# The opening of a convolution and gated projection kernel: earlier casts, copies split by token blocks, and unit 1 convolved in other PSUM banks

## The chip, the cores and the metric

The kernel runs on one core of one Trainium2 chip. The metric is the device time of one execution in microseconds (us); the profile's span, from the first to the last instruction, is about 2 us shorter. In the text PE is TensorE, PEld its weight loads, ACT ScalarE, DVE VectorE, POOL GpSimd, and SP the engine whose queue issues most DMAs. [...]

## The reference

```python
# x: 8 x 4096 x 192, weight: 8 x 7, w_in: 192 x 2048, w_out: 2048 x 192
w = softmax(weight)                                  # per head, over 7 taps
x_pad = concatenate([zeros(B, 6, D), x], axis=1)
attn[b, s, h, :] = sum_k w[h, k] * x_pad[b, s + k, h, :]    # causal convolution, 24 channels a head
h = attn.reshape(32768, 192) @ w_in
out = (h * cos(h)) @ w_out                           # 32768 x 192, float32
```

## The kernel before

**Tiles and units.** The 32,768 tokens are cut into 32 units of 1,024 tokens and 64 tiles of 512 (`T`). A unit is loaded and convolved as a whole and feeds two tiles. The convolution is a matrix product: for each head a band matrix (`band`, 128 x 256 for the current block of 128 tokens and the block before it) holds the softmaxed taps on its diagonals. Its result `ct` has tokens on partitions; it is cast to bf16, doubled so that both halves of the partitions hold it after transposing (`double_unit`, on POOL), and transposed by DMA (`turn_unit`) into `cT`, with channels on partitions.

**A tile.** `mm1(t, j)` (L313) makes two of the sixteen blocks of 128 hidden features in a buffer `h` of two PSUM banks, from six matmuls. `gcu` (L325) takes the cosine on ACT (L327, a sine with a shifted phase) and the product with h on DVE (L331). `mm2_step` (L337) multiplies the products of the tile before by `w_out`, in the banks `o_ps0` and `o_ps1`; `evac` copies them out on ACT, and `store` sends them to memory.

**PSUM.** `h_pool` is a ring of three buffers of two banks; the other two banks are `o_ps0` and `o_ps1`. In the kernel before, the convolution takes its buffers from the h ring (L217).

**Order by hand.** Each engine works its instructions in the order in which the code gives them; waits come from the data dependencies and from buffers that have to come free. In a tile, `PE_ORDER` and `ACT_ORDER` (L368) spell the order: hN is mm1 of pair N, mN are N steps of the second projection, c1 and c2 (for tile 0 also d1 and d2) are the two halves of the matmuls of a half unit's convolution (`conv_part`, L214), sN is `gcu` of pair N, ec and ed are the copies of that convolution's result into `ct`, and | is the middle, at which transposes, stores and loads are issued. Tiles 0 and 1 have orders of their own (L371). In tile 0 the whole of unit 1 is convolved: d is its heads 0 to 3, c its heads 4 to 7. Behind its | come `double_unit(1)` and the casts of unit 2 to bf16 (`cast_unit`, L172: three instructions, and a copy of the margin, L181). In tile 1, c is the first half of unit 2.

**The opening.** While the first loads run, PE does matmuls on zeros (`keep_warm`, L93). ACT and DVE compute the softmax of the taps; DVE multiplies it with a mask into `prod` (L137) and adds seven planes of it (L140); eight copies of 32 partitions each, shared by DVE, ACT and POOL, bring the result into `band` (L147). Then x of unit 0 is cast, the first half on ACT, the second on POOL (L185 to L187). `conv_first` convolves unit 0 in two halves of four blocks: in each half and for each group of four heads, ACT copies one bank of the result into `ct` and DVE the other (`conv_out`, L204). The first half is transposed on PE (`turn_first`, L276), the second by DMA. Then the first half of w_in is cast (L297, one third on each of POOL, DVE and ACT), and the remaining casts go to POOL: the other half of w_in (L303), x of unit 1, and w_out (L306).

Of the kernel before, what the change touches and what calls it, by code (L numbers as in the profile page):

```python
# [8 lines left out]
FP32 = mybir.dt.float32  # L9
BF16 = mybir.dt.bfloat16  # L10
AF = mybir.ActivationFunctionType
ALU = mybir.AluOpType
# [4 lines left out]
def kernel(  # L17
# [8 lines left out]
    nc = tc.nc  # L26
    B, S, D = x.shape
    H, K = weight.shape
    Dff = moe_w_in.shape[1]
    G = D // H  # L30
    NTOK = B * S
    T = 512
    NT = NTOK // T
    NB = T // 128
    U = 1024
    NU = NTOK // U
    UB = U // 128
# [4 lines left out]
    NC = D // 64  # L42
    R = G // NC
# [3 lines left out]
    consts = ctx.enter_context(tc.tile_pool(name="consts", bufs=1))  # L47
# [7 lines left out]
    h_pool = ctx.enter_context(tc.tile_pool(name="h_ps", bufs=3, space=PSUM))  # L55
    o_pools = [ctx.enter_context(tc.tile_pool(name=n, bufs=1, space=PSUM)) for n in ("o_p", "o_q")]
# [18 lines left out]
    w_f = consts.tile([128, NC, NP, 128], FP32)  # L75
# [38 lines left out]
    for q in range(1, 4):  # L114
# [17 lines left out]
    winv = consts.tile([128, H, 1], FP32)  # L132
    nc.vector.reciprocal(winv, wsum)
    nc.vector.tensor_tensor(out=wn, in0=wexp, in1=winv.to_broadcast([128, H, K]), op=ALU.mult)

    prod = consts.tile([128, K, H, E], BF16)
    nc.vector.tensor_tensor(out=prod, in0=mask.rearrange("p k (o e) -> p k o e", o=1).to_broadcast([128, K, H, E]),  # L137
                            in1=wn.rearrange("p h (k o) -> p k h o", o=1).to_broadcast([128, K, H, E]), op=ALU.mult)
    for d, n, m in ((0, 3, 3), (0, 1, 1), (2, 1, 4), (0, 1, 2)):
        nc.vector.tensor_tensor(out=prod[:, d : d + n], in0=prod[:, d : d + n], in1=prod[:, d + m : d + m + n], op=ALU.add)  # L140


    copies = [nc.vector.tensor_copy, nc.scalar.copy, nc.gpsimd.tensor_copy]
    for odd in range(2):
        for q in range(4):
            e0 = 32 * (q ^ (2 * odd))
            copies[(4 * odd + q) % 3](out=band[32 * q : 32 * q + 32, odd:H:2, e0 : e0 + E],  # L147
                                      in_=prod[32 * q : 32 * q + 32, 0, odd:H:2, :])

    w = consts.tile([128, NC, NP, 128], BF16)  # L150
    wo = consts.tile([128, NP, 2, D], BF16)

# [19 lines left out]
    def cast_unit(u, n0=0, n1=UB):  # L172
        copy = nc.scalar.copy if u == 0 and n0 == 0 else nc.gpsimd.tensor_copy
        if u == 0:
            bf[u] = xb0
        else:
            bf[u] = xbf_pool.tile([128, UB + 1, D], BF16, name="x_bf")
            if u % UPS == 0:
                nc.gpsimd.memset(bf[u][:, 0, :], 0.0)
            else:  # L180
                nc.gpsimd.tensor_copy(out=bf[u][:, 0, :], in_=bf[u - 1][:, UB, :])  # L181

        o = bf[u][:, n0 + 1 : n1 + 1, :].rearrange("p n (h t k r) -> t p (n h) k r", t=2, k=NC, r=R)
        i = x_tiles[u][:, n0:n1, :].rearrange("p n (h t r k) -> t p (n h) k r", t=2, k=NC, r=R)
        copy(out=o[0], in_=i[0])  # L185
        copy(out=o[1, 0:64], in_=i[1, 64:128])  # L186
        copy(out=o[1, 64:128], in_=i[1, 0:64])  # L187
        bf.pop(u - 2, None)

    ct_tiles = {}  # L190

    def conv_view(ps, n):

        return ps[:, :, 0 : n * 2 * G].rearrange("p b (n k i r) -> p b i n k r", n=n, k=NC, i=2)

    def conv_mm(u, c, pv, i, rows, prev, n0, n1, **flags):
        h = 4 * c + i
        return nc.tensor.matmul(  # L198
            out=pv[:, i // 2, i % 2],
            lhsT=band[rows, h, 128 if prev else 0 : 256 if prev else 128],  # L200
            rhs=bf[u][rows, n0 + 1 - prev : n1 + 1 - prev, h * G : (h + 1) * G].rearrange("p n (k r) -> p n k r", k=NC),
            skip_group_check=True, **flags)

    def conv_out(u, c, ps, n0, n1, copies, double=False):  # L204
        for b in range(2):
            w0 = (2 * c + b) * 2 * R
            o = ct_tiles[u][:, n0:n1, :, :, w0 : w0 + 2 * R].rearrange("p n k t w -> p (n k) t w")
            i = ps[:, b, 0 : (n1 - n0) * 2 * G].rearrange("p (m t w) -> p m t w", t=1, w=2 * R)
            if double:
                copies[b](o, i.to_broadcast([128, (n1 - n0) * NC, 2, 2 * R]))  # L210
            else:
                copies[b](o[:, :, 0, :], i[:, :, 0, :])  # L212

    def conv_part(u, c, n0=0, n1=UB):  # L214


        ps = h_pool.tile([128, 2, T], FP32, name="h")  # L217
        pv = conv_view(ps, n1 - n0)
        sides = [slice(0, 64), slice(64, 128)]

        def mm(i, rows, prev=0, **flags):
            return conv_mm(u, c, pv, i, sides[rows], prev, n0, n1, **{"start": False, "stop": False, **flags})


        mm(0, 0, start=True)
        mm(2, 1, start=True)
        mm(1, 0)
        mm(2, 1, 1)
        m = mm(1, 0, 1)
        turn = Turn()  # L230
        turn.mark(m, mm(3, 1))
        yield
        m = mm(2, 0)
        turn.wait(m, mm(0, 1))
        mm(3, 0)
        mm(0, 1, 1)
        mm(3, 0, 1, stop=True)
        mm(1, 1, stop=True)
        yield
        if c == 0 and u not in ct_tiles:  # L240
            ct_tiles[u] = ct_pool.tile([128, UB, NC, 2, 64], BF16, name="ct")
        conv_out(u, c, ps, n0, n1, [nc.scalar.copy] * 2)
        yield

    cT = {}
# [13 lines left out]

    cast_unit(0, 0, NB)  # L260
    cast_unit(0, NB, UB)
    ct_tiles[0] = ct_pool.tile([128, UB, NC, 2, 64], BF16, name="ct")
    cT[0] = cT_pool.tile([128, UB, NC, 128], BF16, name="cT")
    copies = [nc.scalar.copy, nc.vector.tensor_copy]

    def conv_first(n0, n1):
        for c in range(2):
            ps = h_pool.tile([128, 2, T], FP32, name="h")
            for i in range(4):
                for prev in range(2):  # L270
                    conv_mm(0, c, conv_view(ps, NB), i, slice(0, 128), prev, n0, n1,
                            start=prev == 0 and i % 2 == 0, stop=prev == 1)
            yield
            conv_out(0, c, ps, n0, n1, copies, double=n0 == 0)

    def turn_first(half):  # L276
        ps = h_pool.tile([128, 2, T], FP32, name="h")
# [14 lines left out]
    list(b)  # L292
    for half in range(2):
        list(across[half])
    cast = [nc.gpsimd.tensor_copy, nc.vector.tensor_copy, nc.scalar.copy]
    for k in range(NC):
        cast[k](out=w[:, k, 0:HP], in_=w_f[:, k, 0:HP])  # L297
    double_unit(0, NB, UB)
    turn_unit(0, NB, UB)
    for q in range(2):  # L300
# [67 lines left out]
    PE_ORDER = "h0 c1 m8 c2 h1 m8 h2 h3 m16 | h4 h5 m8 h6 m12 h7 m12"  # L368
    ACT_ORDER = "P s0 ec s1 s2 s3 Q s4 s5 s6 s7"

    PE_FIRST = ["h0 h1 h2 h3 h4 h5 h6 d1 h7 d2 c1 c2 |", "h0 m8 h1 m8 h2 h3 m16 | h4 c1 h5 m8 c2 h6 m12 h7 m12"]  # L371
    ACT_FIRST = ["s0 s1 s2 s3 s4 s5 s6 ed s7 ec", "s0 s1 s2 s3 s4 s5 ec s6 s7"]

    for t in range(NT + 2):
        u, second = divmod(t, TPU)
        cu, cc = (u + 2, 0) if second else (u + 1, 1)
        conv = {"c": conv_part(cu, cc) if cu < NU else iter(())}
        if t == 0:
            conv["d"] = conv_part(1, 0)
        act, done, h, step = (ACT_ORDER if t > 1 else ACT_FIRST[t]).split(), set(), {}, 0  # L380

        def flush():
            while act:
                k = act[0]
                need = {"P": "start", "Q": "|", "e": k[1:] + "2"}.get(k[0], "h" + k[1:])
                if need not in done:
                    return
                act.pop(0)
                if k == "P" and 0 <= t - 2 < NT:
                    evac(t - 2, 0)  # L390
                elif k == "Q" and 0 <= t - 2 < NT:
                    evac(t - 2, 1)
                elif k[0] == "e":
                    next(conv[k[1]], None)
                elif k[0] == "s" and t < NT:
                    gcu(t, int(k[1:]), h.pop(int(k[1:])))

        done.add("start")
        flush()
        for k in (PE_ORDER if t > 1 else PE_FIRST[t]).split():  # L400
            if k[0] == "h" and t < NT:
                h[int(k[1:])] = mm1(t, int(k[1:]))
            elif k[0] in conv:
                next(conv[k[0]], None)
            elif k[0] == "m":
                for q in range(step, step + int(k[1:])):
                    mm2_step(t, q)
                step += int(k[1:])
            done.add(k)
            flush()  # L410

            if k == ("|" if t == 0 else "h1") and second == 0 and cu < NU:
                double_unit(cu)
            if k == "|":
                if second == 0 and cu < NU:
                    turn_unit(cu)
                if 0 <= t - 2 < NT:
                    store(t - 2)
                if second == 1 and u + 3 < NU:
                    load_unit(u + 3)  # L420
                if second == 0 and u + 2 < NU:
                    cast_unit(u + 2)
# [30 lines left out]
```

## Time and profile before

The time is 740.4 us, the median of three executions from 740.13 to 740.62; the profiled execution has a span of 738.2 us at a granted PE clock of 0.998.

| engine | busy, us | share of the span |
|---|---|---|
| PE | 723.3 | 98% |
| DVE | 620.2 | 84% |
| ACT | 626.8 | 85% |
| POOL | 177.7 | 24% |

The opening in the timelines:

| what | from, us | to, us |
|---|---|---|
| prod and its adds on DVE (L137, L140) | 5.02 | 8.99 |
| copies into band on three engines (L147) | 9.02 | 10.0 |
| casts of unit 0 (ACT; POOL runs beside it from 9.86) | 10.03 | 12.17 |
| convolution of unit 0 without a stop (L198) | 12.22 | 14.29 |
| casts of w_in's first half on ACT, then DVE (L297) | 15.50 | 17.62 |
| first projection (L321), but for two matmuls at 16.25 | 17.68 | |
| first product on DVE (L331) | 19.55 | |

A line of a timeline or of a group of instructions gives the start and the time in us, the engine, the line of the program, the operation, what it writes and reads with the shapes, and the number of instructions joined in it. In square brackets stands how long the engine had been idle before, and which instruction it waited for. A busy time is an average over stages with different limits; the chain of waits says what the end hung on.

### The profile page before, as it was taken

The page shows a single profiled execution, that of the slowest core. Times are in us where ns is not written, and L with a number is a line of the kernel's source. Part 1 is how long each engine was busy: PE and PEld are TensorE (multiplying, and loading weights), DVE is VectorE, ACT ScalarE, POOL GpSimd, SP SyncE. Part 2 cuts the span into 40 slices and gives each one's busy share as a digit, 9 for nine tenths or more (in the row PEclk, how much of TensorE's full clock was granted, in tenths as well). Part 3 has the DMA queues.
Part 4 walks back from the last instruction along what each step waited for, and adds up shares of the span by engine and source line. Part 5 has one row for each costly group of instructions (what it writes and reads, how often), then busy time and mean ns, then how long its engine had stood idle before and what let it go on. Part 6 is the DMA issues. An engine that isn't in the chain of part 4 may idle for free.

```text
span 738.2 us, 26755 instructions
## 1 busy us (share of the span) xinstructions
PE 723.3 (98%) x12073; PEld 553.9 (75%) x12073; DVE 620.2 (84%) x534; ACT 626.8 (85%) x781; POOL 177.7 (24%) x177
## 2 busy tenths in 40 slices
PE   6899999999999999999999999999999999999997
PEld 2477777777777777777777777777777777777776
DVE  6788888888888888888888888888888888888883
ACT  4788888888888888888888888888888888888883
POOL 5622202222212222212222202222212222211000
PEclk9999999999999999999999999999999999999999
DMA  7644244344255354244245244244245455333301
GB/s 188 176 109 112 84 130 119 79 131 117 80 130 125 72 129 124 77 127 129 74 124 130 76 122 129 78 119 130 77 119 131 83 114 114 101 112 87 88 24 66
DMA packets 167940, 79.96 MB, mean 108 GB/s; under 512 B 99474, under 2 KB 167058, under 8 KB 167826
## 3 DMA queue, kind: packets, MB, share of 16 engines
q1 hardware_dynamic: 167824, 78.26, 40.6%
q8 instruction: 94, 1.54, 0.9%
q14 instruction: 20, 0.16, 0.1%
q10 hardware_dynamic: 2, 0.00, 0.0%
HBM read 28.31 MB, written 25.17 MB: 72 GB/s over the span
## 4 chain that ended last, share of the span: by engine, by line
PE 94%; ACT 0%; issue 0%; SPq 0%
PE o_ps L347 46%; PE h L321 44%; PE h L198 4%; ACT o_sb L359 0%; SPq L161 0%
## 5 line engine op out<-in xcount | busy, mean ns | idle before, releaser
L331 DVE TENSOR_TENSOR g<-h,cs 128x1024 bf16<-128x1024 f32 x512 | 609.0, 1220 | 99.1 <-ACT cs L327 90.4
L327 ACT ACTIVATE cs<-h 128x1024 bf16<-128x1024 f32 x512 | 511.6, 1025 | 79.3 <-PE h L321 77.9
L347 PEld LDWEIGHTS <-g 64*128 64x128 bf16 x8192 | 362.1, 94 | 67.4 <-SPq L161 1.8
L347 PE MATMUL o_ps<-wo,g 64*128 64x192 bf16 x8192 | 409.0, 243 | 1.2 <-ACT o_sb L359 1.2
L321 PE MATMUL h<-cT,w 64*128 64x512 bf16 x3072 | 402.9, 377 | 4.1 <-DVE g L331 1.7
L321 PEld LDWEIGHTS <-w 64*128 64x128 bf16 x3072 | 166.1, 94 | 89.0 <-issue 6.4
L249 POOL COPY ct<-ct 128x1536 bf16<-128x1536 bf16 (+1 forms) x32 | 46.2, 1444 | 495.5 <-issue 489.4
L359 ACT COPY o_sb<-o_ps 128x384 f32<-128x384 f32 x128 | 61.3, 479 | 10.9 <-PE o_ps L347 8.2
L212 ACT CAST ct<-h 128x384 bf16<-128x384 f32 (+1 forms) x126 | 54.0, 480 | 11.0 <-PE h L198 7.1
L198 PE MATMUL h<-x_bf,band 64*128 64x192 bf16 (+1 forms) x776 | 55.3, 241 | 4.1 <-ACT x_bf L185 1.7
L198 PEld LDWEIGHTS <-band 64*128 64x128 bf16 (+1 forms) x776 | 38.0, 94 | 17.6 <-issue 3.2
L186 POOL CAST x_bf<-x_f 64x768 bf16<-64x768 f32 (+1 forms) x32 | 38.7, 1208 | 2.0
L187 POOL CAST x_bf<-x_f 64x768 bf16<-64x768 f32 (+1 forms) x32 | 38.5, 1204 | 1.9
L185 POOL CAST x_bf<-x_f 128x768 bf16<-128x768 f32 (+1 forms) x32 | 38.9, 1217 | 0.1
L95 PE MATMUL o_ps<-zero 128*128 128x512 bf16 x19 | 7.3, 554 | 1.3 <-DVE zero L90 1.3
L181 POOL COPY x_bf<-x_bf 128x192 bf16<-128x192 bf16 x24 | 8.4, 350 | 0.0
L95 PEld LDWEIGHTS <-zero 128*128 128x128 bf16 x19 | 2.3, 129 | 5.0 <-issue 3.2
L210 DVE CAST ct<-h 128x384 bf16<-128x384 f32 x2 | 1.0, 553 | 3.3 <-ACT ct L210 3.3
L147 ACT COPY band<-prod 32x152 bf16<-32x152 bf16 x3 | 0.9, 316 | 3.4 <-DVE prod L140 3.3
L306 POOL CAST wo<-wo_f 128x1536 bf16<-128x1536 f32 x2 | 2.9, 1466 | 2.3 <-DMA wo_f<-in_moe_w_out_dram 2.3
L137 DVE TENSOR_TENSOR prod<-mask,wn 128x2128 bf16<-128x2128 bf16 x1 | 2.4, 2376 | 0.1
L98 ACT ACT_TABLE_LOAD x1 | 1.3, 1283 | 1.3 <-PEq L437 1.3
(41 smaller groups left out, 24.4 us busy)
## 6 DMA issues: line engine op xcount, KB each, us to landing
out_dram<-o_sb SPq DMA_DIRECT2D x64, 384.0 KB, 2.9
x_f<-in_x_dram SPq DMA_DIRECT2D x31, 768.0 KB, 5.2
w_f<-in_moe_w_in_dram SPq DMA_DIRECT2D x4, 384.0 KB, 7.7
wo_f<-in_moe_w_out_dram SPq DMA_DIRECT2D x4, 384.0 KB, 5.0
x_f<-in_x_dram SPq DMA_DIRECT2D x2, 384.0 KB, 4.0
cT<-ct SPq DMA_TRANSPOSE x32, 4.8
w_row<-in_weight_dram ACTq DMA_DIRECT2D x1, 0.2 KB
```

The lines of the kernel that those rows point to most:

```text
L95: nc.tensor.matmul(out=idle, lhsT=zero[:, 0:128], rhs=zero, start=True, stop=True)
L185: copy(out=o[0], in_=i[0])
L186: copy(out=o[1, 0:64], in_=i[1, 64:128])
L187: copy(out=o[1, 64:128], in_=i[1, 0:64])
L198: return nc.tensor.matmul(out=pv[:, i // 2, i % 2], lhsT=band[rows, h, 128 if prev else 0 : 256 if prev else 128], rhs=bf[u][rows, n0 + 1 ...
L212: copies[b](o[:, :, 0, :], i[:, :, 0, :])
L249: nc.gpsimd.tensor_copy(out=ct[:, n0:n1, :, 1, :], in_=ct[:, n0:n1, :, 0, :])
L321: nc.tensor.matmul(out=h[:, i, :], lhsT=w[rows, k, j, :], rhs=c[rows, n0 : n0 + NB, k, :], start=(k == 0), stop=(k == NC - 1))
L327: nc.scalar.activation(out=cs, in_=h, func=AF.Sin, bias=math.pi / 2.0, scale=1.0)
L331: nc.vector.tensor_tensor(out=g_tiles[t][:, 2 * j : 2 * j + 2, :], in0=h, in1=cs, op=ALU.mult)
L347: m = nc.tensor.matmul(out=o_ps[tt, b][:, si * D : (si + 1) * D], lhsT=g_tiles[tt][rows, f, s * 128 : (s + 1) * 128], rhs=wo[rows, f // 2, ...
L359: nc.scalar.copy(o_sb[t][:, 2 * b : 2 * b + 2, :].rearrange("p s d -> p (s d)"), o_ps.pop((t, b))[:, 0 : 2 * D])
```

## The change

It has four parts, all ahead of tile 2. The casts of unit 0 stand in the program ahead of `prod`, its adds and the copies into `band`, so that they can run while DVE makes these. The casts of w_in's first half follow the copies into `band` at once, ahead of the convolution of unit 0. Its result is copied into `ct` by token blocks: ACT takes blocks 0 and 1 of each half with both banks, DVE blocks 2 and 3, so that each PE transpose of two blocks needs one engine's copies. And unit 1 is convolved in the two o banks, which stand idle during tile 0, instead of in h buffers; its halves are placed earlier among the projections, and c can begin only when the copies of d have left the banks. The second projection of tile 0, which begins in tile 1, needs the same banks when the copies of c have left them.

```diff
-    prod = consts.tile([128, K, H, E], BF16)
-    nc.vector.tensor_tensor(out=prod, ...)
...
     cast_unit(0, 0, NB)
     cast_unit(0, NB, UB)
+
+    prod = consts.tile([128, K, H, E], BF16)
+    nc.vector.tensor_tensor(out=prod, in0=mask.rearrange("p k (o e) -> p k o e", o=1).to_broadcast([128, K, H, E]),
+                            in1=wn.rearrange("p h (k o) -> p k h o", o=1).to_broadcast([128, K, H, E]), op=ALU.mult)
+    for d, n, m in ((0, 3, 3), (0, 1, 1), (2, 1, 4), (0, 1, 2)):
+        nc.vector.tensor_tensor(out=prod[:, d : d + n], in0=prod[:, d : d + n], in1=prod[:, d + m : d + m + n], op=ALU.add)
...
+    three = [nc.vector.tensor_copy, nc.scalar.copy, nc.gpsimd.tensor_copy]
+    for odd in range(2):
+        for q in range(4):
+            e0 = 32 * (q ^ (2 * odd))
+            three[(4 * odd + q) % 3](out=band[32 * q : 32 * q + 32, odd:H:2, e0 : e0 + E],
+                                     in_=prod[32 * q : 32 * q + 32, 0, odd:H:2, :])
+    for k in range(NC):
+        three[(k + 2) % 3](out=w[:, k, 0:HP], in_=w_f[:, k, 0:HP])
...
     def conv_first(n0, n1):
         for c in range(2):
-            ps = h_pool.tile([128, 2, T], FP32, name="h")
+            ps = ring_banks()
...
-            conv_out(0, c, ps, n0, n1, copies, double=n0 == 0)
+            for half in range(2):
+                conv_out(0, c, ps, n0, n0 + 2 * half, n0 + 2 * half + 2, copies[half], double=n0 == 0)
...
-    cast = [nc.gpsimd.tensor_copy, nc.vector.tensor_copy, nc.scalar.copy]
-    for k in range(NC):
-        cast[k](out=w[:, k, 0:HP], in_=w_f[:, k, 0:HP])
...
+    def ring_banks():
+        h = h_pool.tile([128, 2, T], FP32, name="h")
+        return [h[:, 0, :], h[:, 1, :]]
+
+    def o_banks():
+        return [o_pools[b].tile([128, T], FP32, name="o_ps%d" % b) for b in range(2)]
...
-    PE_FIRST = ["h0 h1 h2 h3 h4 h5 h6 d1 h7 d2 c1 c2 |", "h0 m8 h1 m8 h2 h3 m16 | h4 c1 h5 m8 c2 h6 m12 h7 m12"]
-    ACT_FIRST = ["s0 s1 s2 s3 s4 s5 s6 ed s7 ec", "s0 s1 s2 s3 s4 s5 ec s6 s7"]
+    PE_FIRST = ["h0 h1 h2 h3 h4 d1 h5 d2 h6 c1 h7 c2 |", "h0 m8 h1 m8 h2 h3 m16 | h4 c1 h5 m8 c2 h6 m12 h7 m12"]
+    ACT_FIRST = ["s0 s1 s2 s3 s4 s5 ed s6 s7 ec", "s0 s1 s2 s3 s4 s5 ec s6 s7"]
...
-        conv = {"c": conv_part(cu, cc) if cu < NU else iter(())}
+        conv = {"c": conv_part(cu, cc, ring_banks if t else o_banks) if cu < NU else iter(())}
         if t == 0:
-            conv["d"] = conv_part(1, 0)
+            conv["d"] = conv_part(1, 0, o_banks)
```

More of the change, by code (lines that the diff above doesn't have):

```diff
@@ L134 @@
     nc.vector.tensor_tensor(out=wn, in0=wexp, in1=winv.to_broadcast([128, H, K]), op=ALU.mult)
-    prod = consts.tile([128, K, H, E], BF16)
[L137 to L148, printed above, removed]
     w = consts.tile([128, NC, NP, 128], BF16)
@@ L190, with conv_mm @@
     ct_tiles = {}
-    def conv_view(ps, n):
-        return ps[:, :, 0 : n * 2 * G].rearrange("p b (n k i r) -> p b i n k r", n=n, k=NC, i=2)
-    def conv_mm(u, c, pv, i, rows, prev, n0, n1, **flags):
+    def conv_mm(u, c, ps, i, rows, prev, n0, n1, **flags):
         h = 4 * c + i
         return nc.tensor.matmul(
-            out=pv[:, i // 2, i % 2],
+            out=ps[i // 2][:, 0 : (n1 - n0) * 2 * G].rearrange("p (n k i r) -> p i n k r", n=n1 - n0, k=NC, i=2)[:, i % 2],
             lhsT=band[rows, h, 128 if prev else 0 : 256 if prev else 128],
@@ L202, in conv_mm, with conv_out, conv_part @@
             skip_group_check=True, **flags)
-    def conv_out(u, c, ps, n0, n1, copies, double=False):
+    def conv_out(u, c, ps, n0, m0, m1, copy, double=False):
         for b in range(2):
             w0 = (2 * c + b) * 2 * R
-            o = ct_tiles[u][:, n0:n1, :, :, w0 : w0 + 2 * R].rearrange("p n k t w -> p (n k) t w")
-            i = ps[:, b, 0 : (n1 - n0) * 2 * G].rearrange("p (m t w) -> p m t w", t=1, w=2 * R)
+            o = ct_tiles[u][:, m0:m1, :, :, w0 : w0 + 2 * R].rearrange("p n k t w -> p (n k) t w")
+            i = ps[b][:, (m0 - n0) * 2 * G : (m1 - n0) * 2 * G].rearrange("p (m t w) -> p m t w", t=1, w=2 * R)
             if double:
-                copies[b](o, i.to_broadcast([128, (n1 - n0) * NC, 2, 2 * R]))
+                copy(o, i.to_broadcast([128, (m1 - m0) * NC, 2, 2 * R]))
             else:
-                copies[b](o[:, :, 0, :], i[:, :, 0, :])
-    def conv_part(u, c, n0=0, n1=UB):
-        ps = h_pool.tile([128, 2, T], FP32, name="h")
-        pv = conv_view(ps, n1 - n0)
+                copy(o[:, :, 0, :], i[:, :, 0, :])
+    def ring_banks():
[3 more added lines that the diff above has]
+        return [o_pools[b].tile([128, T], FP32, name="o_ps%d" % b) for b in range(2)]
+    def conv_part(u, c, banks):
+        ps = banks()
         sides = [slice(0, 64), slice(64, 128)]
         def mm(i, rows, prev=0, **flags):
-            return conv_mm(u, c, pv, i, sides[rows], prev, n0, n1, **{"start": False, "stop": False, **flags})
+            return conv_mm(u, c, ps, i, sides[rows], prev, 0, UB, **{"start": False, "stop": False, **flags})
         mm(0, 0, start=True)
@@ L241, in conv_part @@
             ct_tiles[u] = ct_pool.tile([128, UB, NC, 2, 64], BF16, name="ct")
-        conv_out(u, c, ps, n0, n1, [nc.scalar.copy] * 2)
+        conv_out(u, c, ps, 0, 0, UB, nc.scalar.copy)
         yield
@@ L267, in conv_first @@
         for c in range(2):
-            ps = h_pool.tile([128, 2, T], FP32, name="h")
+            ps = ring_banks()
             for i in range(4):
                 for prev in range(2):
-                    conv_mm(0, c, conv_view(ps, NB), i, slice(0, 128), prev, n0, n1,
-                            start=prev == 0 and i % 2 == 0, stop=prev == 1)
+                    conv_mm(0, c, ps, i, slice(0, 128), prev, n0, n1, start=prev == 0 and i % 2 == 0, stop=prev == 1)
             yield
-            conv_out(0, c, ps, n0, n1, copies, double=n0 == 0)
+            for half in range(2):
+                conv_out(0, c, ps, n0, n0 + 2 * half, n0 + 2 * half + 2, copies[half], double=n0 == 0)
     def turn_first(half):
```

## The prediction

> **What bounds the kernel now.** I read the chain of work that ended last first, because it says from which moment one engine alone sets the end. Its pieces from the start to 60 us are these (start us, us, what):
>
> ```profile
> by line: PE h L321 19.0%; PE o_ps L347 18.6%; PE h L198 2.5%; issue 0.1%
> 35.97 0.04 issue
> 36.01 0.24 PE h L198
> ...
> 44.39 1.38 PE h L321 x12
> ...
> 55.43 1.38 PE h L321 x12
> ```
>
> Nothing stands in it before 35.97, and from 36.01 to the end it is TensorE without a gap: one tile of 512 tokens every 55.43 - 44.39 = 11.04 us. So the time is "the moment at which TensorE becomes saturated" plus a fixed 702 us. The change touches only what lies before it; each us by which that moment moves is a us of the result, and nothing later can hide it. The timeline of TensorE says what it waited for last:
>
> ```profile
> 36.01 0.24 PE L198 MATMUL h<-x_bf,band 64*128 64x192 bf16 x1 [0.32 <-POOL x_bf L187]
> 36.11 0.82 PE L321 MATMUL h<-cT,w 64*128 64x512 bf16 x6
> ```
>
> That is the convolution of unit 2 in tile 1, waiting for the third cast of unit 2 on GpSimd. The timeline of GpSimd follows it back, and those of ACT and DVE follow the rest:
>
> ```profile
> 30.50 1.47 POOL L249 COPY ct<-ct 128x1536 bf16<-128x1536 bf16 x1 [3.70 <-ACT ct L212]
> 31.91 0.35 POOL L181 COPY x_bf<-x_bf 128x192 bf16<-128x192 bf16 x1
> ...
> 34.75 1.21 POOL L187 CAST x_bf<-x_f 64x768 bf16<-64x768 f32 x1
> ```
>
> ```profile
> 19.55 8.31 DVE L331 TENSOR_TENSOR g<-h,cs 128x1024 bf16<-128x1024 f32 x7 [1.93 <-ACT cs L327]
> 29.71 1.23 DVE L331 TENSOR_TENSOR g<-h,cs 128x1024 bf16<-128x1024 f32 x1 [1.85 <-ACT cs L327]
> 31.40 4.66 DVE L331 TENSOR_TENSOR g<-h,cs 128x1024 bf16<-128x1024 f32 x4 [0.46 <-ACT cs L327]
> ```
>
> ```profile
> 27.89 0.86 ACT L212 CAST ct<-h 128x384 bf16<-128x384 f32 x2 [1.49 <-PE h L198]
> 28.64 1.04 ACT L327 ACTIVATE cs<-h 128x1024 bf16<-128x1024 f32 x1
> 29.56 0.88 ACT L212 CAST ct<-h 128x384 bf16<-128x384 f32 x2
> ```
>
> Two chains meet at 36. One: the last copy out of unit 1's convolution ends at 30.44, then GpSimd doubles (1.47), copies the margin and casts unit 2 (5.5 us in all, to 35.96). Two: DVE's products, 1.19 us each, whose fourth of tile 1 ends at 31.40 + 4.66 = 36.06 and frees the buffer that h5 takes at 36.11. Both start from the first product at 19.55. Ahead of it, the opening:
>
> ```profile
> 16.13 1.49 DVE L297 CAST w<-w_f 128x512 bf16<-128x512 f32 x1
> ```
>
> The first projection runs from 17.68, when this cast has ended; its first cosine starts at 18.50.
>
> **What the Trainium skill says.** "SBUF — State Buffer", section "Who interferes with whom": DVE shares one port pair with GpSimd under an exclusive lock; a DVE copy in a two-port mode, or a DVE instruction with two SBUF inputs against a GpSimd instruction that reads SBUF, shuts the other out for the whole instruction. The trace agrees for copies: the DVE cast of L297 took 1.49 us where ACT needed 0.62 for the same size, and it ended 0.27 us after the GpSimd cast of L303 (15.88 to 17.35). No row shows the two-input case: GpSimd was idle while prod was made. "PSUM — Partial Sum Buffer", section "PSUM bank collisions raise a hardware error": two engines may not be on one bank at once, reads included. In the trace DVE's first ct copy (13.18) starts when ACT's on the same h tile (12.67 + 0.48) has ended, so I keep that order after the change. "TensorE: Matmul & The Clock Gate", section "What's actually happening": the clock falls to half after an idle window of about 3.4 us. The trace has 0.50 from 18.0 to 21.0.
>
> **Part 1, the x casts go ahead of prod and the band copies.** Before, band copies end at 10.0, then three casts of 0.70 on ACT and of 0.68 on GpSimd, and the convolution runs from 12.22. After, x's first half has landed by 4.1 (issued 0.74, 3.4 to land), ACT is free at 5.7, so ACT casts until 7.8 in idle time: free. GpSimd's half lands by 5.9, while DVE is in prod (L137, 5.02 to 7.40, two SBUF inputs). Not locked, GpSimd casts until 8.0 for nothing, the band is ready at 10.0 as before, and the convolution gains 2.1 us. Locked, GpSimd waits until 7.40, and then its three casts (2.05) and DVE's four adds (1.56) share one port: 7.40 + 3.61 = 11.0. Band copies (1.0) end at 12.1. If DVE wins each time, GpSimd's two band copies stand behind its own casts and end near 12.3. Either way the convolution starts at 12.1 to 12.3, and the gain is gone. I take locked, as the page calls this case measured.
>
> **Part 2, w's first-half casts go ahead of the convolution's copies.** DVE's 1.49 us before the projection go. They now follow the band copies: ACT 0.62 (12.1 to 12.7), GpSimd 0.62, DVE about 0.35 behind GpSimd's (to 12.9). w_f's first two loads land at 7.9 and 9.5, so no wait. Queued behind these casts are the ct copies, whose input is ready at about 12.65: 0.1 to 0.2 us of the cost shows.
>
> **Part 3, ct copies by token blocks.** Each engine gets 8 smaller copies instead of 4. From 0.48 and 0.33 (ACT, 384 and 192 elements) and 0.55 and 0.35 (DVE), 96 elements come to 0.25 on each. DVE's chain: first copy 13.4 (behind ACT's pair), four at a pitch of 0.30, four at 0.22, then the transposed copy of 0.96: 13.4 + 1.2 + 0.9 + 1.0 = 16.5. The projection starts at about 16.6, not 17.68. With six matmuls (0.82) the first cosine is at 17.45 and the first product at 18.5, 1.05 us earlier than 19.55.
>
> **Part 4, unit 1's convolution in the o banks.** It no longer takes h buffers, and d stands after h4 instead of h6. Before, ACT sat 1.49 us before the ct copies at 27.89, and DVE 1.85 us before its eighth product. Followed from 18.5: h4 ends at 21.7 (after the second product, 20.9). d1 wants unit 1's casts: doubling of unit 0 at 15.5, 0.8, L303 1.47, margin 0.35, casts 3.75, so 22.0, when h5's buffer frees anyway (22.1). d2 ends at 23.6. ACT: s5 to 24.3, the two copies to 25.2, s6 to 26.2 (DVE idle 0.5), s7 to 27.2, the last copies to 28.1. c1 waits for the first pair of copies, a new wait of TensorE with h7 behind it: h7 ends at 26.2, in time for s7. The first m8 of tile 1 waits for the o bank until 28.1, with h1 behind it: h1 ends at 29.1, in time. So the last ct copy ends at 28.1 to 28.2 instead of 30.44, GpSimd's 5.5 us bring unit 2's cast to 33.7, and DVE's products of tile 1 run from 29.2, the fourth ending at 33.95. h5 starts at about 34.0 instead of 36.11: 2.1 us, of which 1.05 from the opening and 1.05 from tile 0. The removed DVE idle (2.3) exceeds this because 0.5 comes back before s6 and 0.7 at the tile's edge. 740.4 - 2.1 = 738.3.
>
> **Rivals.**
> The casts are not locked out by prod: the convolution starts at 10.05, ACT's w cast ends at 10.65, DVE's chain goes from 11.3 to 14.4, and the first product is at 16.3. Part 4 then gains some 0.6, as d1 has to wait for unit 1's cast (20.1, since its x lands only at 15.1). 3.2 + 0.6: 736.6. For it: no row shows this lock. Against: the page, and the lock on copies in the trace.
>
> No change to be measured: the lock holds, and the half clock falls on the projection's start: six matmuls take 1.28 instead of 0.82 (as from 18.5 to 19.7 before), and the ring runs at 1.28 instead of 1.19 for three steps. That takes 0.7 us; if the tile's edge also costs what h1 behind m8 may cost (0.3), 1.1 us are left: 739.3. For it: such a dip is in the trace at that place. Against: the projection starts before 18, and ring steps are bound by DVE.
>
> Slower: the lock costs more than one port's sum, say the band at 12.9 because copies on DVE and GpSimd collide too, the projection at 17.7, and unit 1's cast at 23.5, so that d1 holds h5 back by 1.5 us where d once stood behind h6. With the edge at 0.7 and the half clock at 0.7 that is 2.9 against the 1.05 of part 4: 742.2. For it: d1 sits in order ahead of h5, h6 and h7, and its margin is near nothing. Against: h0 to h4 keep ACT and DVE fed for five steps.
>
> **How the numbers follow.** Forecast 0.55, not locked 0.20, no change 0.17, slower 0.08. The range runs from 736.0 (the case without the lock, 736.6, with 0.6 for its copies) to 740.0 (the half clock, 739.3, with 0.7 for a second step of it); outside lie the slower case and a tail of some 0.05 on each side. Faster by over 0.2% means under 738.9. The forecast lies 0.6 us inside that, so 0.05 of it goes to "same"; of the half-clock case, which lies 0.4 outside, 0.04 comes back. Faster 0.74, same 0.18, slower 0.08.
>
> **What would show it.** In the profile of the changed kernel: ACT's x casts between 5.7 and 7.8; GpSimd's x casts stretched, or DVE's four adds (1.56 us) spread, until about 11; the convolution from about 12.1 (10.05 if not locked); no DVE cast ahead of the projection, which starts near 16.6; DVE's eight products of tile 0 in about 10 us with one gap near 0.5; the chain of waits starting near 34 and 11.04 us a tile after it. I am wrong if the chain starts before 33 or after 35.5, if d1 waits long for x_bf, or if the period of 11.04 moves.

## The result, and the profile after

The changed kernel takes 737.41 us (median of four executions, 737.10 to 737.99), the kernel before beside it 740.26 (739.83 to 740.62). The ratio is 0.9963, with a 95% interval from 0.9945 to 0.998: 1.5 to 4.1 us faster, where 2.1 were forecast (the ratio sets all executions of one kernel against all of the other, not median against median). All line numbers below are those of the changed kernel unless said otherwise.

The chain of work that ended last, after (start us, us, what):

```profile
34.25 0.04 issue
34.29 0.24 PE h L180
34.53 0.65 PE h L324 x6
...
42.47 1.38 PE h L324 x12
...
53.51 1.38 PE h L324 x12
```

It has the shape of before, TensorE alone and 53.51 - 42.47 = 11.04 us a tile, and it starts 1.72 us earlier. As a mark for all kernels here I take the first row of twelve projections, at 44.39 before and 42.47 after. From it to the end of the span are 693.8 us before and 693.7 after. Nothing behind the mark has moved by more than 0.1 us; the 1.92 us between the marks are the gain of this profiled execution.

The opening on DVE, GpSimd and ACT, after (timelines of single engines):

```profile
5.02 2.38 DVE L253 TENSOR_TENSOR prod<-mask,wn 128x2128 bf16<-128x2128 bf16 x1
7.43 2.81 DVE L256 TENSOR_TENSOR prod<-prod 128x912 bf16<-128x912 bf16 x4
10.28 0.79 DVE L263 COPY band<-prod 32x152 bf16<-32x152 bf16 x3
11.10 0.87 DVE L266 CAST w<-w_f 128x512 bf16<-128x512 f32 x1
```

```profile
5.73 2.22 POOL L170 CAST x_bf<-x_f 128x384 bf16<-128x384 f32 x1 [2.00 <-DMA x_f<-in_x_dram]
8.01 0.98 POOL L171 CAST x_bf<-x_f 64x384 bf16<-64x384 f32 x1
9.04 0.68 POOL L172 CAST x_bf<-x_f 64x384 bf16<-64x384 f32 x1
```

```profile
5.60 0.70 ACT L170 CAST x_bf<-x_f 128x384 bf16<-128x384 f32 x1
6.31 0.71 ACT L171 CAST x_bf<-x_f 64x384 bf16<-64x384 f32 x1
7.03 0.70 ACT L172 CAST x_bf<-x_f 64x384 bf16<-64x384 f32 x1
```

GpSimd's first cast and the four adds before the change, each while the other of the two engines was idle:

```profile
7.43 1.56 DVE L140 TENSOR_TENSOR prod<-prod 128x912 bf16<-128x912 bf16 x4
9.86 0.68 POOL L185 CAST x_bf<-x_f 128x384 bf16<-128x384 f32 x1
```

ACT's casts run in idle time, as forecast, and GpSimd is held up, as forecast for a locked port. Its first cast took 2.22 us where the same cast took 0.68 before, and it ended 0.55 us behind prod's end; the four adds took 2.81 us instead of 1.56. But they were done at 10.24 and not at 11.0. On TensorE:

```profile
11.36 1.44 PE L180 MATMUL h<-x_bf,band 128*128 128x96 bf16 x22 [0.27 <-ACT band L263]
13.15 0.80 PE L180 MATMUL h<-x_bf,band 128*128 128x96 bf16 x8 [0.35 <-DVE ct L193]
13.75 1.48 PE L286 MATMUL h<-ident,ct 128*128 128x128 bf16 x12
16.37 2.12 PE L324 MATMUL h<-cT,w 64*128 64x512 bf16 x18 [1.14 <-DVE cT L290]
```

The convolution starts at 11.36 instead of 12.22, and it waits once for a copy of its result, 0.35 us, as it did before (0.48 us, from 13.31 to 13.79; it did not run without a stop there). The projection starts at 16.37 instead of 17.68. The twelve transposes took 1.48 us where they took 0.84 before:

```profile
14.26 0.84 PE L280 MATMUL h<-ident,ct 128*128 128x128 bf16 x12
```

In this execution the half clock fell there, from 12 to some 15.3 us. Two rows of the view of the clock (stretch, its length, PE's busy time, granted clock, share and GB/s of the DMA):

```profile
12.00:13.00 1.00, 0.80 (x11) 0.50 1.12 172
16.00:17.00 1.00, 0.63 (x6) 1.00 0.00 0
```

Tile 0 and the hand-over to tile 1, on DVE, GpSimd and ACT:

```profile
18.29 6.88 DVE L334 TENSOR_TENSOR g<-h,cs 128x1024 bf16<-128x1024 f32 x6 [2.06 <-ACT cs L330]
25.43 2.46 DVE L334 TENSOR_TENSOR g<-h,cs 128x1024 bf16<-128x1024 f32 x2 [0.26 <-ACT cs L330]
28.34 4.96 DVE L334 TENSOR_TENSOR g<-h,cs 128x1024 bf16<-128x1024 f32 x4 [0.46 <-ACT cs L330]
```

```profile
27.36 1.47 POOL L309 CAST wo<-wo_f 128x1536 bf16<-128x1536 f32 x1 [3.14 <-DMA wo_f<-in_moe_w_out_dram]
28.77 1.47 POOL L238 COPY ct<-ct 128x1536 bf16<-128x1536 bf16 x1
```

```profile
26.53 0.86 ACT L195 CAST ct<-o_ps 128x384 bf16<-128x384 f32 x2
```

DVE's idle time of 1.85 us in tile 0 has shrunk to 0.26. The lines of GpSimd and ACT show something that the forecast did not have: the last copy of unit 1 into ct ended at 26.53 + 0.86 = 27.39, but its doubling began at 28.77. In front of it in GpSimd's queue stood the second cast of w_out, which had waited 3.14 us for its load.

### The profile page after: what moved, and what is told of

Read it like the earlier page. It is cut to its first block, busy times and chain, and to the rows that moved or that the text cites. A ratio compares the mean times of both kernels' runs of the same rounds, so it can differ in the third digit from the quotient of the medians.

```text
span 736.2 us, 26768 instructions
## 1 busy us (share of the span) xinstructions
PE 720.7 (98%) x12073; PEld 554.7 (75%) x12073; DVE 621.1 (84%) x538; ACT 626.8 (85%) x785; POOL 179.2 (24%) x177
## 4 chain that ended last, share of the span: by engine, by line
PE 95%; ACT 0%; issue 0%; SPq 0%
PE o_ps L350 46%; PE h L324 45%; PE h L180 4%; ACT o_sb L362 0%; SPq L146 0%
## 5 line engine op out<-in xcount | busy, mean ns | idle before, releaser
L195 ACT CAST ct<-h 128x384 bf16<-128x384 f32 (+1 forms) x124 | 52.4, 474 | 9.8 <-PE h L180 5.9
L170 POOL CAST x_bf<-x_f 128x768 bf16<-128x768 f32 (+1 forms) x32 | 40.4, 1262 | 2.0 <-DMA x_f<-in_x_dram 2.0
L256 DVE TENSOR_TENSOR prod<-prod 128x304 bf16<-128x304 bf16 (+1 forms) x4 | 2.7, 705 | 0.1
L180 PE MATMUL o_ps<-x_bf,band 64*128 64x192 bf16 x24 | 2.0, 242 | 0.5 <-ACT ct L195 0.3
```

Source lines behind the costliest of these rows:

```text
L180: return nc.tensor.matmul(out=ps[i // 2][:, 0 : (n1 - n0) * 2 * G].rearrange("p (n k i r) -> p i n k r", n=n1 - n0, k=NC, i=2)[:, i % 2], ...
L195: copy(o[:, :, 0, :], i[:, :, 0, :])
```

## The experiments

Each was timed against the kernel before on the same chip. That gave 740.26 us beside "part 4 alone" and parts 4, 1 and 2 undone; 740.42 beside "taps in PSUM", "unit 0 cast on ACT", "w_out loaded early" and both; and 740.43 beside the other four. Kernels of different groups are compared by their ratios. Mark, first projection and first product (us) are from the one execution that was profiled, with the mean clock granted in it. That mean is a rough sign only, as it also counts half clock behind the last matmul (up to 3.4 us), where it costs nothing: with part 3 undone the whole opening ran at full clock, at a mean of 0.998, and the changed kernel had 3.4 us of half clock in it, at 0.997.

| kernel | median us | ratio, 95% interval | projection | product | mark | clock |
|---|---|---|---|---|---|---|
| before | 740.26 | | 17.68 | 19.55 | 44.39 | 0.998 |
| changed | 737.41 | 0.9963, 0.9945 to 0.998 | 16.37 | 18.29 | 42.47 | 0.997 |
| changed again | 737.81 | 0.9964, 0.9951 to 0.9976 | 16.39 | 18.94 | 42.27 | 0.993 |
| part 4 alone | 738.88 | 0.9979, 0.9971 to 0.9988 | 17.89 | 20.02 | 43.35 | 0.993 |
| part 4 undone | 738.26 | 0.9974, 0.9963 to 0.9984 | 16.43 | 18.98 | 43.66 | 0.995 |
| part 1 undone | 738.67 | 0.9977, 0.9967 to 0.9987 | 17.22 | 19.13 | 42.61 | 0.998 |
| part 2 undone | 737.99 | 0.9968, 0.9956 to 0.9979 | 17.22 | 19.36 | 42.70 | 0.996 |
| part 3 undone | 736.78 | 0.9953, 0.994 to 0.9965 | 15.40 | 17.32 | 40.61 | 0.998 |
| taps in PSUM | 737.18 | 0.9956, 0.9944 to 0.9969 | 15.89 | 18.45 | 41.78 | 0.993 |
| unit 0 cast on ACT | 737.37 | 0.9954, 0.9941 to 0.9968 | 16.02 | 18.58 | 41.91 | 0.993 |
| w_out loaded early | 737.82 | 0.9957, 0.9945 to 0.997 | 16.28 | 18.83 | 42.30 | 0.994 |
| PSUM and w_out | 736.39 | 0.9952, 0.9939 to 0.9964 | 14.88 | 16.79 | 40.07 | 0.998 |
| changed, zeros | 736.52 | 0.9955, 0.9943 to 0.9968 | 15.68 | 17.60 | 41.00 | 0.999 |
| all three | 736.16 | 0.9947, 0.9934 to 0.9961 | 14.90 | 16.81 | 40.39 | 0.999 |

**Part 4 alone**, that is, the kernel before with these lines:

```diff
-    PE_FIRST = ["h0 h1 h2 h3 h4 h5 h6 d1 h7 d2 c1 c2 |", ...]
-    ACT_FIRST = ["s0 s1 s2 s3 s4 s5 s6 ed s7 ec", ...]
+    PE_FIRST = ["h0 h1 h2 h3 h4 d1 h5 d2 h6 c1 h7 c2 |", ...]
+    ACT_FIRST = ["s0 s1 s2 s3 s4 s5 ed s6 s7 ec", ...]
-        conv = {"c": conv_part(cu, cc) if cu < NU else iter(())}
+        conv = {"c": conv_part(cu, cc, ring_banks if t else o_banks) if cu < NU else iter(())}
...
-            conv["d"] = conv_part(1, 0)
+            conv["d"] = conv_part(1, 0, o_banks)
```

> The kernel before with the fourth part alone (unit 1 convolved in the o banks, new orders of tile 0). My theory: the opening and the order of tile 0 each give about half of the 2 us by which the chain of waits starts earlier, so this kernel takes 739.2 to 739.5 where the kernel before takes 740.3, its first product still begins at 19.5 us, and the last copies of unit 1 into ct end about 1 us earlier than 30.4. Rival A (all of it is the order of tile 0): 737.5 to 738. Rival B (all of it is the opening, the order gives nothing): 740.1 to 740.4.

The ratio gives 0.9 to 2.1 us, by the medians 1.4: the gain is clear of zero, and a little larger than expected (738.88, where 739.2 to 739.5 were expected). The last copies of unit 1 ended at 29.27, 1.2 us earlier. The profiled execution was at half clock for over 6 us of the opening, so its first product was 0.5 us later than before; its mark was still 1.04 earlier. From first product to mark it needs 43.35 - 20.02 = 23.3 us, the kernel before 24.8: part 4 saves 1.5 us on that way. Its two halves, the banks and the places in the order, were not tried apart.

**Part 4 undone**, the first three parts alone (the same lines the other way round in the changed kernel).

> The changed kernel with the fourth part undone (unit 1 convolved in the h ring, orders of tile 0 as before), so the first three parts alone. My theory: first product at 18.3 us, DVE again idle for 1.5 to 2.3 us in tile 0, 738.6 to 739.2. Rival A (the order gives all): 740.0 to 740.4. Rival B (the opening gives all): 737.2 to 737.8.

DVE's gap of 1.85 us in tile 0 is back, and from product to mark it takes 24.7 us as before:

```profile
28.99 1.23 DVE L334 TENSOR_TENSOR g<-h,cs 128x1024 bf16<-128x1024 f32 x1 [1.85 <-ACT cs L330]
```

By the medians 2.0 us are gained. Rival A falls. The median, 738.26, lies between the theory and rival B, and the interval (1.2 to 2.7 us gained) does not part the two; what speaks against B is the kernel with part 4 alone, which gains by itself. The two halves, 1.4 and 2.0, come to more than the whole, 2.6 to 2.85.

**Part 1 undone.**

```diff
-    cast_unit(0, 0, NB)
-    cast_unit(0, NB, UB)
-
     prod = consts.tile([128, K, H, E], BF16)
...
                                      in_=prod[32 * q : 32 * q + 32, 0, odd:H:2, :])
+    cast_unit(0, 0, NB)
+    cast_unit(0, NB, UB)
     for k in range(NC):
```

> The changed kernel with the casts of unit 0 behind the copies into band, as before, but ahead of the casts of w_in. My theory (GpSimd and DVE shut each other out while prod is added up, which gives back half of what the early casts bring): the four adds take 1.56 us again instead of 2.81, the band is ready at 10.0, the convolution starts at 12.2 instead of 11.4, and the time is 0.7 to 1.0 us above the changed kernel's. Rival (the lock takes all): no difference. Rival (the early casts are free): 2 us above.

The timeline of DVE in this kernel:

```profile
7.42 1.56 DVE L253 TENSOR_TENSOR prod<-prod 128x912 bf16<-128x912 bf16 x4
9.02 0.82 DVE L260 COPY band<-prod 32x152 bf16<-32x152 bf16 x3
```

The adds are at 1.56 us again, as expected, the convolution starts at 12.21, and the ratio is 0.9977 against 0.9963 and 0.9964: 1.0 us by the ratios, though the intervals overlap. The whole kernel gives 0.86 us at the convolution's start (11.36 for 12.22); so the early casts bring about 0.9 us there and not 2.1, because the adds, stretched by 1.25 us, take the rest.

**Part 2 undone.**

```diff
-    for k in range(NC):
-        three[(k + 2) % 3](out=w[:, k, 0:HP], in_=w_f[:, k, 0:HP])
...
+    cast = [nc.gpsimd.tensor_copy, nc.vector.tensor_copy, nc.scalar.copy]
+    for k in range(NC):
+        cast[k](out=w[:, k, 0:HP], in_=w_f[:, k, 0:HP])
     double_unit(0, NB, UB)
```

> The changed kernel with the casts of the first half of w_in where they were before, behind the convolution of unit 0. My theory: DVE's cast takes about 1.5 us again beside GpSimd's large cast and stands ahead of the first projection, which starts at about 17.5 instead of 16.4: 0.8 to 1.2 us above the changed kernel. Rival (that wait is taken over by something else at the same place, the half clock or the transposed copy): less than 0.4 us above.

DVE's cast takes 1.63 us and ends at 17.16, and the projection starts at 17.22, 0.3 us earlier than expected:

```profile
15.53 1.63 DVE L301 CAST w<-w_f 128x512 bf16<-128x512 f32 x1
```

The time lies 0.2 us above one timing of the changed kernel and 0.6 above the other; by the ratios it is 0.3 to 0.4 us, which is the rival's range, and the intervals overlap: no gain of part 2 is shown in the time. This profiled execution had the half clock for 3.4 us, the changed kernel's second one for some 6.8, and the first product came only 0.42 us later than there (19.36 against 18.94); the mark follows it by 0.43. So the wait is in the trace. That its cost depends on where the half clock falls is a reading of these two profiles and was not tested.

**Part 3 undone**: `copies[b]` takes bank b, all four blocks of it.

```diff
-                copy(o, i.to_broadcast([128, (m1 - m0) * NC, 2, 2 * R]))
+                (copy[b] if isinstance(copy, list) else copy)(o, i.to_broadcast([128, (m1 - m0) * NC, 2, 2 * R]))
...
-            for half in range(2):
-                conv_out(0, c, ps, n0, n0 + 2 * half, n0 + 2 * half + 2, copies[half], double=n0 == 0)
+            conv_out(0, c, ps, n0, n0, n1, copies, double=n0 == 0)
```

> The changed kernel with the third part undone: ACT copies bank 0 of unit 0's convolution and DVE bank 1, as before. My theory (the split adds as many instruction costs as it saves in waits): first projection at 16.2 to 16.7 us as in the changed kernel, and the time within 0.4 us of the anchor's. Rival (the split is what shortens the opening): first projection past 17.0 and 0.6 us or more above.

The rival falls, but the theory was off too: the first projection comes at 15.40 and not at 16.2 to 16.7, a us earlier than with the split, and the median is 1.0 us below the changed kernel beside it; the intervals overlap. The timelines of DVE, first in this kernel and then in the changed kernel with the zeros (below), which was at full clock too; in both the convolution starts at 11.38:

```profile
12.34 1.02 DVE L193 CAST ct<-h 128x384 bf16<-128x384 f32 x2 [0.36 <-ACT ct L193]
13.28 0.35 DVE L195 CAST ct<-h 128x192 bf16<-128x192 f32 x1
13.84 0.36 DVE L195 CAST ct<-h 128x192 bf16<-128x192 f32 x1 [0.21 <-ACT ct L195]
14.30 0.96 DVE L289 CAST cT<-h 128x768 bf16<-128x768 f32 x1
```

```profile
12.41 1.15 DVE L193 CAST ct<-h 128x192 bf16<-128x192 f32 x4 [0.42 <-ACT ct L193]
13.48 0.41 DVE L195 CAST ct<-h 128x96 bf16<-128x96 f32 x2
14.13 0.42 DVE L195 CAST ct<-h 128x96 bf16<-128x96 f32 x2 [0.24 <-ACT ct L195]
14.57 0.96 DVE L290 CAST cT<-h 128x768 bf16<-128x768 f32 x1
```

With eight small copies the transposed copy begins 0.27 us later than with four larger ones, and in both DVE waits for ACT: the order between two engines on one PSUM tile was not removed by the split. That accounts for 0.27 of the us; the other 0.7 in the traces is the half clock, which did not fall on the opening in this execution (with the split, the projection comes at 15.68 at full clock and at 16.37 with the half clock). So the split costs about 0.3 us at one and the same clock; in the medians this is not apart from the scatter.

**Taps in PSUM.** prod's second input comes from free columns of the bank that held the broadcast taps, in float32.

```diff
-    wn = consts.tile([128, H, K], BF16)
+    wn = w_all[:, 64 : 64 + H * K].rearrange("p (h k) -> p h k", k=K)
```

> The changed kernel with the softmaxed taps in PSUM (float32, in free columns of the bank that held the broadcast taps) instead of SBUF, so that prod has one SBUF input and not two. My theory (two SBUF inputs on DVE shut GpSimd's casts out): GpSimd's first cast of unit 0 takes 0.7 us instead of 2.22, all three are done by about 7.9, the adds take under 2.1 us instead of 2.81, the band is ready by 10.4 instead of 11.3, and the time is 0.5 to 1.0 us below the changed kernel's. Rival (GpSimd's first cast was long for another reason, such as its data landing late): 2.2 us again and the same time.

The timeline of GpSimd in this kernel; prod takes 2.37 us, from 5.03 to 7.40:

```profile
6.50 0.70 POOL L170 CAST x_bf<-x_f 128x384 bf16<-128x384 f32 x1 [2.77 <-DMA x_f<-in_x_dram]
7.27 0.70 POOL L171 CAST x_bf<-x_f 64x384 bf16<-64x384 f32 x1
8.01 1.00 POOL L172 CAST x_bf<-x_f 64x384 bf16<-64x384 f32 x1
```

This speaks for the lock and against the rival. The first cast begins in the middle of prod and takes 0.70 us, although its data landed 0.8 us later here. With the taps in SBUF it began anywhere from 5.33 to 6.03 us in the kernels of this study and always ended between 7.94 and 7.97. The edit changes the input's type as well as its place (float32 for bf16), and no run parts the two; prod itself took as long as before. The adds, which still read two SBUF inputs, took 2.32 us; in the kernel with both changes, where x landed at 5.84, 2.03.

**Unit 0 cast on ACT.**

```diff
-        copy = nc.scalar.copy if u == 0 and n0 == 0 else nc.gpsimd.tensor_copy
+        copy = nc.scalar.copy if u == 0 else nc.gpsimd.tensor_copy
```

> The changed kernel with both halves of unit 0 cast on ACT, so that GpSimd does nothing beside prod and the adds. My theory: the adds take 1.56 us again and end at 9.0; ACT's six casts end at 9.8 and its band copies at 10.8, so the convolution starts at 10.9 instead of 11.4, and the time is 0.3 to 0.6 us below the changed kernel's. Rival (the adds are slow for another reason than GpSimd): 2.8 us again, and a time equal or above.

The adds are at 1.56 again, as expected, and the band is ready at 10.9; the convolution starts at 11.0. Both kernels, this one and the one with the taps in PSUM, start the projection 0.4 to 0.5 us earlier than the changed kernel. Their ratios are lower than its by 0.0007 to 0.001, which the intervals do not separate.

**w_out loaded early.**

```diff
     wo_src = moe_w_out.rearrange("(i j p) d -> p j i d", i=2, p=128)
+    for q in range(2):
+        for i in range(2):
+            nc.sync.dma_start(out=wo_f[:, q * HP : (q + 1) * HP, i], in_=wo_src[:, q * HP : (q + 1) * HP, i])
...
     turn_unit(0, NB, UB)
-    for q in range(2):
-        for i in range(2):
-            nc.sync.dma_start(out=wo_f[:, q * HP : (q + 1) * HP, i], in_=wo_src[:, q * HP : (q + 1) * HP, i])
```

> The changed kernel with the loads of w_out issued behind the load of unit 1 instead of behind unit 0's DMA transposes. In the changed kernel GpSimd's second cast of w_out waits 3.1 us for its load until 27.4 us and holds up the doubling of unit 1, whose input is ready at 27.4, until 28.8. My theory: that wait goes, the doubling starts at 27.4, TensorE is saturated at 33.2 to 33.4 instead of 34.3 (there DVE's products take over), and the time is 0.8 to 1.1 us below the changed kernel's. Rival (DVE's products bind there as much): 0.2 or less below. Rival (the loads push unit 1's x back, which lands at 15.9 us and is needed at 17.4): above.

The wait is gone (the casts of w_out run from 21.15 to 24.03), but the median, 737.82, is no lower; the ratio is, by 0.4 to 0.5 us, and its interval overlaps. In the second profile of the changed kernel the w_out cast had ended at 27.13, ahead of the doubling's input, so the load is late in some executions only. What held TensorE last in that profile was DVE, which the forecast had at 33.95:

```profile
31.75 2.37 DVE g L334 x2
34.11 0.04 issue
34.15 0.82 PE h L324 x6
```

The traces also show what the late load costs. In four profiles the doubling began behind the cast of w_out, 1.38, 0.68, 0.59 and 0.48 us after the last copy into ct (changed, part 1 undone, zeros, part 3 undone; elsewhere 0.05 to 0.06). From first product to mark these took 24.2, 23.5, 23.4 and 23.3 us. So about 0.5 us of delay is hidden behind DVE's products, and what lies above it is paid. The five executions of this kernel fall in two groups by the clock: 737.82 to 737.89 at 0.993 and 0.994, 736.28 and 736.30 at 1.0 and 0.998. The changed kernel gave 737.1 at 1.0. This fits two chains, DVE's products at half clock and the load at full clock, but single executions without a profile do not show it.

**Both** edits, taps in PSUM and w_out loaded early.

> Both: taps in PSUM and w_out loaded early. My theory: the two gains add up, 1.3 to 2.0 us below the changed kernel. Rival (one chain binds behind the other, so that they do not add): no better than the better of the two.

736.39 at 0.9952, 0.8 to 0.9 us below the changed kernel by the ratios, less than the 1.3 to 2.0 expected, and lower than either alone, with intervals that overlap. Here too the executions fall in two groups: 735.72 and 735.77 at a clock of 0.998, 737.94 and 738.14 at 0.993. With the taps in PSUM alone the two clocks differ little (736.78 to 737.18 at 0.999 and 1.0, 737.33 and 737.43 at 0.993 and 0.994), as they would where the late load takes back what the clock gives; no profile shows that kernel at full clock. In the profile, with full clock throughout the opening, the mark is 2.4 us earlier than the changed kernel's, and what held TensorE last was no longer GpSimd but DVE:

```profile
29.54 2.37 DVE g L334 x2
31.90 0.04 issue
31.95 0.82 PE h L324 x6
```

Followed further back, the chain goes over the first half of unit 1's convolution (20.36) and GpSimd's casts of unit 1 to the load of its x, which was issued at 4.44 and landed at 16.46, 0.6 us later than in the changed kernel:

```profile
4.44 12.03 DMA x_f<-in_x_dram
```

So with the other losses gone the opening hangs on a load that the forecast named only for its rival without a lock.

**The changed kernel again**, with no edit.

> The changed kernel itself, beside the other three on one chip. In five traces of the opening variants TensorE's clock was at half for 3.4 us and in others for 6.8 us, at different places. My theory: part of the scatter of the changed kernel's times (737.1 to 738.0) is this, and the kernel takes 737.0 to 738.0 again. Rival (another chip state made the difference): a median outside that.

737.05 to 737.95 with a median of 737.81, as expected; the granted clock was 0.993 to 0.996.

**The changed kernel with zeros.**

```diff
+    keep_warm(9)
     list(conv_first(0, NB))
...
     for half in range(2):
         list(across[half])
+    keep_warm(5)
```

> The changed kernel with 9 more matmuls on zeros ahead of the convolution of unit 0 and 5 ahead of the first projection, in time in which TensorE waits. My theory (idle time in the opening lowers the clock, and the transposes of unit 0, 1.48 us at half clock and 0.84 at full, stand on the path): the clock stays at 1.0, the first product begins at 17.5 to 17.8 us, and the time is 0.6 to 1.0 us below the anchor's. Rival (the half clock is hidden behind DVE and ACT): the same time within 0.3. Rival (the zeros stand in the way): above.

The clock is 0.999 in all five executions, the transposes take 0.83 us, and the first product begins at 17.60; the median is 1.3 us below the kernel beside it, more than the 0.6 to 1.0 expected, and the intervals overlap. Three executions lie at 736.3 to 736.5 and two at 737.8 and 738.5, at the same clock. What held those two is open: a late w_out load would do it, but neither was profiled.

**All three** (taps in PSUM, w_out early, and 6 and 4 matmuls on zeros).

> Taps in PSUM, w_out loaded early, and 6 and 4 more matmuls on zeros. My theory (three separate losses: port, load, clock): first product at 16.8 us in every run, 735.4 to 736.0. Rival (the clock dips for other reasons): 736.4 as without the zeros.

736.16 at 0.9947, the lowest of the study, between the 735.4 to 736.0 expected and the rival's 736.4, 4.3 us under the kernel before by the medians, and 1.2 to 1.3 under the changed kernel by the ratios; the intervals overlap here too. One of five executions, 737.71 at a clock of 0.996, suggests that the zeros did not hold the clock up each time.

## Why the prediction was right

**What bounds.** Right: the time is the moment of saturation plus a constant. From mark to end all fourteen profiles took 693.6 to 693.9 us. The chain was forecast to start at about 34.0 and started at 34.29 in one profile of the changed kernel (GpSimd last); in the other, TensorE waited last at 34.15 (DVE last). Both chains of the forecast are real, and which of them ends last changes from one execution to the next.

**Part 1.** The mechanism was right as far as the runs show it, its size was not. (The sum itself has a slip: 11.0 and 1.0 are 12.0, not 12.1.) The term "casts 2.05 and adds 1.56 on one port, 3.61" measured 2.84 (7.40 to 10.24): the adds grew by 1.25 us and not by 2.05. The convolution started at 11.36, not 12.1. What the Trainium skill says in "SBUF — State Buffer", section "Who interferes with whom", is borne out for a DVE instruction with two SBUF inputs: 2.22 us against 0.70 with one of them in PSUM. That the other engine is shut out for the whole instruction nearly holds for prod: the cast ended 0.55 us behind it and takes 0.68 alone. For the adds, less was lost than whole instructions in turn.

**Parts 2 and 3.** The projection was forecast at 16.6 and came at 16.37. Two errors cancel: 0.74 us from part 1, and the half clock on the transposes (1.48 instead of 0.84), which I had looked for on the projection. That 16.37 lies so near to 16.6 is luck. The split was booked as part of the way to 16.5 and is worth nothing: undone, the opening is no longer, and about 0.3 us shorter at full clock. Part 2 took DVE's cast out from ahead of the projection, as forecast, but by the times its gain is not apart from zero.

**Part 4.** Forecast 1.05 us. By the medians it brings 1.4 us alone and 0.5 to 0.9 on top of the other parts (738.26 to 737.81 or 737.41); from first product to mark it saves 1.5 alone. In the first profile after only 0.7 of that shows: product to mark took 24.2 us there, and 23.3 in the second. The step that the prediction left out is the cast of w_out, which stands ahead of the doubling in GpSimd's order and whose load landed only at 27.3 in the first profile; with "GpSimd's 5.5 us" counted from the last ct copy, the sum took the queue for empty. The new waits were small, but not quite as harmless as worked out: c1 waited 0.35 us for the o banks and the first m8 0.59; ACT then waited 0.21 us for h7 and 0.27 for h1 behind them. DVE followed without a further gap, but sat 0.46 us before the first product of tile 1, as it did before; whether that would be less without the new waits was not tried.

**Sum.** 1.26 us at the first product (forecast 1.05) and 0.66 from there to the mark (forecast 1.05) make the 1.92 of the profile, near the 2.1 by two misses of opposite sign; the medians differ by 2.85. The profiled execution after was the slowest of its four. The others, at clocks of 0.997 to 1.0, took 0.4 to 0.9 us less.

## What to carry to other kernels

Where one engine is saturated to the end, an opening is worth the us by which it moves the start of that saturation (here within 0.3 us in fourteen profiles); find the mark, and compare everything by it. Idle time on GpSimd beside DVE's prod, with two SBUF inputs, was not free for casts (2.22 us for 0.68); with one small input in PSUM, as float32, it was (0.70). When an instruction is moved earlier, look at what stands ahead of the next one in its engine's queue and has its own load to wait for.

## What the runs showed of the hardware

The place and the length of the half clock in the opening differ between executions of one kernel: from 12 to some 15.3 us in one profile of the changed kernel, from 13 to some 19.9 in the other, while the time from the first product to the mark hardly depends on it: with part 4 it was 23.3 to 23.6 us in eleven of twelve profiles, with 6.8 us of half clock as with none; the twelfth, 24.2, is the one with the late load of w_out. In the kernel with w_out loaded early, executions at 0.993 and 0.994 were 1.5 us longer than those at 0.998 and 1.0. That is as much as part 4 alone brought. It is not so in every kernel: with the taps in PSUM the two clocks lie some 0.4 us apart.
